# Loading the first x chunk half by plain load with TensorE transposes and half by a transposing load, with one W1 slab on ScalarE's queue

## The chip, the cores and the metric

The kernel runs on one core of one Trainium2 chip, written directly in Bass: each engine has its own list of instructions, and every order between engines is a semaphore wait. The metric is the device time in microseconds of one execution; before the change it is 147.2 us, the median of 6 runs (146.67 to 147.51).

## The reference

Two branches work on the same x and are mixed by a gate for each row. Cut to what matters:

```python
# x: 2048 x 512 bf16; wqkv: 512 x 1536; w_phi: 32 x 16 x 16; w1: 512 x 1376; w2: 1376 x 512; wo: 512 x 512
g = sigmoid((x * gate_w).sum(-1, keepdims=True))
# a: linear attention, 32 heads of 16
q, k, v = split(x @ wqkv)
pq, pk = q @ w_phi, k @ w_phi                               # for each head
phi_q = concat([softmax(pq), softmax(-pq)])                 # 32 features; phi_k alike
o = (phi_q @ (phi_k.T @ v)) / (phi_q @ phi_k.sum(0) + 1e-6)
a = o @ wo
# b: dense layer with relu
b = relu(x @ w1) @ w2
out = g * a + (1 - g) * b
```

## The kernel before, in words

x is worked on in 4 chunks of 512 rows. TensorE contracts over the partitions, so every product with x needs x transposed: tile XT holds, for each of the four 128-column blocks of x (the contraction slabs, index `dt` or `t`), all 2048 rows along the free dimension. Chunks 1 to 3 arrive in XT by a transposing load (L188). Chunk 0 is needed first and goes another way: four plain loads (L162, semaphores x00 to x03) bring its rows into XS, which is part of tile OT, so that each partition holds one row of each load. TensorE then transposes 16 blocks of 128x128 by a matmul with an identity matrix (`xtr`, L237), and VectorE (L247) and ScalarE (L249) copy the results from PSUM to XT (`xev`). A block (dt, j) is column block dt of the rows of load j. The rows are dealt out as `(p j)`: load j takes rows 4p+j, and the output rows of the first four tiles are stored back by the same rule (`orow`).

The first large piece of TensorE work is the first 8 column units of h = x @ w1 for chunk 0 (`slab`, L520). Here the slab of the contraction is the outer loop: slab(0) runs units 0 to 7 into eight PSUM banks, then slab(1), slab(2) and slab(3) add to them; each is 8 matmuls of 512 columns. Slab t needs W1 rows t*128 to t*128+127 (events w10a, w10, w11, w12, w13; slab 0's row block comes as two halves) and XT's column block t of chunk 0 (events xv..., list `XV`). After slab 3 the relus (L258, L260) free the banks, and the remaining units of W1 (`hunit`, L272), the v tiles (`vtile`, L404) and the folded q/k weights (`pre`, L306) follow without a pause in the order written out by hand.

All loads sit on two queues, each in the order written: SyncE (SP) issues x00, x02, then w10a, w10, w11, w12, w13 (L165), the rest of W1 (w1r, L178), w_phi (wps, L180), the v weights (wv, L182), two transposing loads of the q and k weights (wqk0, wqk1, L185), and the transposing loads of chunks 1 to 3 (x1 to x3, L188). ScalarE (ACT) issues x01, x03 and the gate vector (gr, L170). `warm` (L231) issues matmuls on a constant that keep TensorE busy while the first x rows are on their way. `p.early` places an engine's first instructions ahead of the start barrier.

Of the kernel before, what the change touches and what calls it, by code (L numbers as in the profile page):

```python
# [68 lines left out]
def bass_gated_mix__linear_kernel_hedgehog__dense_activation_relu__prompt_kernel(  # L69
# [11 lines left out]
    x2 = A_x.rearrange("b s d -> (b s) d")  # L81
    o2 = out.rearrange("b s d -> (b s) d")
# [3 lines left out]
    DFF = B_w1.shape[1]  # L86
    P = 128
    NT = S // P
    NDT = D // P
# [15 lines left out]
    with ExitStack() as es:  # L105
        E = es.enter_context
        XT = E(nc.sbuf_tensor("XT", [P, NDT, S], BF16))
# [43 lines left out]
        p = _Plan(["sp", "pool", "act", "dve", "pe"])  # L151
        free = {b: [] for b in range(8)}


        xq = x2[0:512, :].rearrange("(p j) d -> p j d", j=4)
        oq = o2[0:512, :].rearrange("(p j) d -> p j d", j=4)

        def orow(m):
            return oq[:, m, :] if m < 4 else o2[m * P:(m + 1) * P, :]

        def loadx0(j, eng):
            p.dma(eng, lambda e: e.dma_start(out=XS[:, j, :], in_=xq[:, j, :]), f"x0{j}", ev=f"x0{j}")  # L162

        def loadw1(t, c0=0, c1=DFF, tag=""):
            p.dma("sp", lambda e: e.dma_start(  # L165
                out=W1[:, t, c0:c1], in_=B_w1[t * P:(t + 1) * P, c0:c1]), f"w1{t}{tag}", ev=f"w1{t}{tag}")

        for j in range(NDT):
            loadx0(j, ("sp", "act")[j % 2])
        p.dma("act", lambda e: e.dma_start(out=GR[0:NDT, :], in_=gate_w.rearrange("(j p) -> j p", p=P)),  # L170
              "gr", after=["grz"], ev="gr")
        p.early("act")
        p.early("sp")
        loadw1(0, 0, 4 * P, "a")
        loadw1(0, 4 * P, 8 * P)
        for t in range(1, NDT):
            loadw1(t, 0, 8 * P)
        p.dma("sp", lambda e: e.dma_start(  # L178
            out=W1[:, :, 8 * P:DFF], in_=B_w1[:, 8 * P:DFF].rearrange("(j p) n -> p j n", p=P)), "w1r", ev="w1r")
        p.dma("sp", lambda e: e.dma_start(  # L180
            out=WPS[:, :, :], in_=A_w_phi.rearrange("(g hl) r c -> (hl r) g c", g=NDT)), "wps", ev="wps")
        p.dma("sp", lambda e: e.dma_start(  # L182
            out=WV[:, :, :], in_=A_wqkv[:, 2 * D:3 * D].rearrange("(j p) n -> p j n", p=P)), "wv", ev="wv")
        for i in range(2):
            p.dma("sp", lambda e, i=i: e.dma_start_transpose(  # L185
                out=WQKT[:, 4 * i:4 * i + 4, :], in_=A_wqkv[:, i * D:(i + 1) * D]), f"wqk{i}", ev=f"wqk{i}")
        for c in range(1, NCH):
            p.dma("sp", lambda e, c=c: e.dma_start_transpose(  # L188
                out=XT[:, :, c * 512:(c + 1) * 512], in_=x2[c * 512:(c + 1) * 512, :]), f"x{c}", ev=f"x{c}")
# [9 lines left out]
            after=["wps"], ev="wd")  # L199
        for gt in range(NDT):  # L200
# [4 lines left out]
                after=["wd", "m8"], ev=f"wbd{gt}")  # L205
# [11 lines left out]
             after=["r64"], ev="m32")  # L217

        def xready(c):
            return [f"xv{n}" for n in ("a0", "a1", "a2", "c0", "d0", "b1", "b3")] if c == 0 else [f"x{c}"]  # L220

        def gatecol(bank):
            gp = PS[:, bank, 0:NDT]
# [5 lines left out]
        def warm(n, cols=512):  # L229
            for _ in range(n):  # L230
                p.op("pe", lambda e: e.matmul(PS[:, 4, 0:cols], ones[:, 0:P], ones[:, 0:cols], start=True, stop=True),  # L231
                     after=["one"])

        def xtr(nm, blocks, bank, last=True, off=0):
            for i, (dt, j) in enumerate(blocks):
                o = off + i * P
                p.op("pe", lambda e, dt=dt, j=j, o=o: e.matmul(  # L237
                    PS[:, bank, o:o + P], XS[:, j, dt * P:(dt + 1) * P], IDN[:, :], start=True, stop=True),
                    after=["idn", f"x0{j}"] + (free[bank] if o == 0 else []),
                    ev=(f"xt{nm}" if last and i == len(blocks) - 1 else None))  # L240

        def xev(eng, nm, js, dts, bank):
            w = len(js) * P
            d = XT[:, dts[0]:dts[-1] + 1, js[0] * P:js[0] * P + w]
            s = PS[:, bank, 0:len(dts) * w].rearrange("p (t c) -> p t c", c=w)
            if eng == "dve":
                p.op("dve", lambda e: e.tensor_copy(d, s), after=[f"xt{nm}"], ev=f"xv{nm}")  # L247
# [21 lines left out]
        def hunit(c, kt, eng="act", bank=None):  # L269
            bank = nextbank() if bank is None else bank  # L270
            for t in range(NDT):
                p.op("pe", lambda e, t=t: e.matmul(  # L272
                    PS[:, bank, :], W1[:, t, kt * P:(kt + 1) * P], XT[:, t, c * 512:(c + 1) * 512],
                    start=(t == 0), stop=(t == NDT - 1)),
                    after=(xready(c) + w1all + free[bank] if t == 0 else ()),
                    ev=(f"h{c}_{kt}" if t == NDT - 1 else None))
            relu(c, kt, bank, eng)
# [224 lines left out]
        def comb(m, cs=slice(0, 512), tag="", eng="sp"):  # L502
            ob = m % 3
            bank = fbank[(m, tag)]
            n = cs.stop - cs.start
            p.op("dve", lambda e: e.scalar_tensor_tensor(  # L506
                out=OSB[:, ob, cs], in0=PS[:, bank, 0:n], scalar=OMG[:, m:m + 1],
                in1=TFA[:, m % 2, cs], op0=ALU.mult, op1=ALU.add),
                after=[f"fb{m}{tag}", f"ta{m}"] + ([f"out{m - 3}"] if m >= 3 else []), ev=f"cb{m}{tag}")
            free[bank] = [f"cb{m}{tag}"]  # L510
            p.dma(eng, lambda e: e.dma_start(out=orow(m)[:, cs], in_=OSB[:, ob, cs]),
                  f"out{ob}" if m < NT - 3 else "fin", after=[f"cb{m}{tag}"], ev=f"out{m}{tag}")


        UB = (3, 4, 5, 0, 6, 7, 2, 1)
        XV = (("xva0", "xvc0", "xvd0"), ("xva1", "xvb1"), ("xva2", "xvb1"), ("xva2", "xvb3"))

        def slab(t):
            for u in range(8):
                p.op("pe", lambda e, u=u: e.matmul(  # L520
                    PS[:, UB[u], :], W1[:, t, u * P:(u + 1) * P], XT[:, t, 0:512],
                    start=(t == 0), stop=(t == NDT - 1)),
                    after=["w10a" if t == 0 and u < 4 else f"w1{t}", *XV[t]] + (free[UB[u]] if t == 0 else []),
                    ev=(f"h0_{u}" if t == NDT - 1 else None))

        A, B = (0, 1), (2, 3)
        warm(4)
        p.early("pe")
        warm(1, 384)
        xtr("a0", ((0, 0),), 6, last=False)  # L530
        xtr("a1", ((1, 0),), 5, last=False)
        xtr("a2", ((2, 0),), 7, last=False)
        xtr("a2", ((3, 0),), 7, last=False, off=2 * P)
        xtr("a0", ((0, 1),), 6, off=P)
        xtr("a1", ((1, 1),), 5, off=P)
        xtr("a2", ((2, 1),), 7, last=False, off=P)
# [47 lines left out]
        for m in range(NT):  # L584
# [33 lines left out]
        for m in range(NT):  # L618
            if m > 1 and m + 3 < NT:
                nd(m + 3)  # L620
            if m + 1 < NT - 1:
                finB(m + 1, FB[(m + 1) % 3])
            if m == 1:
                nd(m + 3)
            if m == 0:
                nd(2)
                nd(3)
            finA(m, (6, 2, 0)[max(m - NT + 3, 0)])
            if m < NT - 1:
                comb(m)  # L630
        m = NT - 1
# [3 lines left out]
        for i, cs in enumerate(cuts):  # L635
            comb(m, cs, "ab"[i], ("sp", "act")[i])
# [35 lines left out]
```

The softmax here doesn't subtract the row's maximum and nothing guards it: scores larger than these inputs give would overflow.

## Time and profile before

| | |
|---|---|
| runs before | 147.2 us median, 146.67 to 147.51 |
| the profiled execution: its own time | 146.77 us |
| its span, first to last instruction | 145.5 us |
| TensorE (PE) busy | 141.8 us, 97% of the span |
| VectorE (DVE), ScalarE (ACT), GpSimd (POOL) busy | 92.4, 72.7, 52.0 us |
| granted TensorE clock | 1.00 |
| first x load lands, first slab matmul starts | 2.76 us, 4.69 us |
| the slab stage (32 matmuls), then the next group | 4.69 us, 11.75 us |

The page has one line for each engine's busy time, a strip of 40 slices over the span, the DMA queues, the chain of work that ended last, and the costliest groups of instructions with what ended their idle time. "L520" is line 520 of the kernel before. Other views of the same trace used here are the chain in order of time, the waits of one engine, one line's instructions with the time from issue to landing of its DMAs, and the DMA packets in a window. All times are us from the first instruction of the span.

### The profile page before, as it was taken

Reading aid. Unit: us, or ns where it says so; the run is one execution under the profiler, and the core shown is the slowest. Engines: PE = TensorE matmul, PEld = TensorE weight load, DVE = VectorE, ACT = ScalarE, POOL = GpSimd, SP = SyncE. Lnnn points to the kernel's source line nnn. Section 1 sums busy time; section 2 is a strip of 40 time slices with the busy share of each in tenths; the row PEclk is TensorE's granted clock in tenths of the full one; section 3 lists DMA queues with packets and bytes.
Section 4 is the critical chain, followed back from the end, with each engine's and each line's share of the span. In section 5 each row is a group of like instructions: output and inputs, shape, how many; then the busy total and the mean of one; then the engine's idle time right before and its main releaser. Section 6 shows DMA issues by size and latency. Waiting matters only on the chain.

```text
span 145.5 us, 2522 instructions
## 1 busy us (share of the span) xinstructions
PE 141.8 (97%) x960; PEld 72.8 (50%) x977; DVE 92.4 (64%) x158; ACT 72.7 (50%) x125; POOL 52.0 (36%) x62
## 2 busy tenths in 40 slices
PE   8999999999999999999999999999999999999994
PEld 3444744444446555544645555554444444444443
DVE  2528818777686888678698968664455555555342
ACT  3315667779778778797878861022211111111150
POOL 2040004777878668678879810200000000000000
DMA  6999990213459973325734332355242222322213
GB/s 182 312 257 226 267 182 17 54 26 68 72 118 360 147 203 66 71 46 110 77 72 98 82 72 39 75 106 132 53 108 72 72 72 70 79 72 74 72 45 106
DMA packets 45509, 16.12 MB, mean 111 GB/s; under 512 B 39384, under 2 KB 45112, under 8 KB 45496
## 3 DMA queue, kind: packets, MB, share of 16 engines
q1 hardware_dynamic: 45056, 15.65, 48.0%
q10 hardware_dynamic: 440, 0.30, 0.6%
q8 instruction: 8, 0.13, 0.4%
q14 instruction: 5, 0.04, 0.1%
HBM read 4.41 MB, written 2.10 MB: 45 GB/s over the span
## 4 chain that ended last, share of the span: by engine, by line
PE 95%; DMA 2%; DVE 1%; issue 1%; SPq 0%
PE PS L483 26%; PE PS L272 19%; PE PS L328 18%; PE PS L492 9%; PE PS L404 9%; PE PS L520 5%; PE PS L458 3%; PE PS L426 3%; PE PS L284 2%; DMA OT<-in_A_x_dram 2%; PE PS L306 1%; DVE WQK L506 1%; DVE XT L247 1%; PE PS L237 0%; SPq L657 0%
## 5 line engine op out<-in xcount | busy, mean ns | idle before, releaser
L483 PE MATMUL PS<-W,HT 128*128 128x512 bf16 (+3 forms) x182 | 40.2, 366 | 0.3
L372 POOL TENSOR_TENSOR EB<-EB,SC 128x1024 bf16<-128x1024 bf16 x15 | 28.9, 1928 | 23.8 <-DVE SC L370 23.8
L348 ACT ACTIVATE EB<-PS 128x480 bf16<-128x480 f32 (+1 forms) x44 | 30.1, 757 | 14.2 <-PE PS L328 14.2
L497 ACT ACTIVATE TFA<-PS,GT 128x512 bf16<-128x512 f32 x16 | 11.0, 687 | 42.7 <-PE PS L492 36.6
L272 PE MATMUL PS<-XT,W 128*128 128x512 bf16 x124 | 30.2, 379 | 0.2
L328 PE MATMUL PS<-WQK,XT 128*128 128x480 bf16 x128 | 28.5, 366 | 0.0
L368 DVE TENSOR_REDUCE ZB<-EB 128x64 f32<-128x1024 bf16 x15 | 18.3, 1220 | 14.2 <-ACT EB L348 14.2
L506 DVE SCALAR_TENSOR_TENSOR WQK<-PS,OMG,TFA 128x512 bf16<-128x512 f32 (+2 forms) x17 | 12.2, 719 | 23.6 <-ACT TFA L497 22.4
L483 PEld LDWEIGHTS PS<-W,HT 128*128 128x128 bf16 (+1 forms) x187 | 17.0, 98 | 17.4
L258 ACT ACTIVATE HT<-PS 128x512 bf16<-128x512 f32 x35 | 20.3, 616 | 6.8 <-PE PS L520 5.0
L328 PEld LDWEIGHTS PS<-WQK,XT 128*128 128x128 bf16 x128 | 12.5, 98 | 13.6
L383 DVE TENSOR_REDUCE ZB<-EB 128x64 f32<-128x1024 bf16 x16 | 18.7, 1168 | 0.0
L272 PEld LDWEIGHTS PS<-XT,W 128*128 128x128 bf16 x128 | 12.0, 98 | 13.2
L392 POOL TENSOR_TENSOR EB<-EB,SC 128x512 bf16<-128x512 bf16 x16 | 16.9, 1055 | 1.3
L492 PE MATMUL PS<-WO,OT 128*128 128x512 bf16 x62 | 16.0, 378 | 0.1
L404 PE MATMUL PS<-WV,XT 128*128 128x512 bf16 x59 | 15.3, 378 | 0.3
L468 DVE TENSOR_TENSOR WQK<-PS,RDEN 128x512 bf16<-128x512 f32 x16 | 11.1, 691 | 0.6
L492 PEld LDWEIGHTS PS<-WO,OT 128*128 128x128 bf16 x64 | 6.1, 97 | 7.2
L414 ACT ACTIVATE VS<-PS 128x512 bf16<-128x512 f32 x14 | 8.5, 610 | 2.0 <-PE PS L404 2.0
L370 DVE RECIPROCAL SC<-ZB 128x64 f32<-128x64 f32 x16 | 8.8, 553 | 0.5
L404 PEld LDWEIGHTS PS<-WV,XT 128*128 128x128 bf16 x64 | 5.4, 97 | 4.8
L458 PEld LDWEIGHTS PS<-KVNZ,PHQ 128*128 128x128 bf16 x128 | 6.1, 97 | 3.6
(57 smaller groups left out, 86.8 us busy)
## 6 DMA issues: line engine op xcount, KB each, us to landing
out_dram<-WQK SPq DMA_DIRECT2D x15, 128.0 KB, 1.7
W<-in_B_w_dram SPq DMA_DIRECT2D x3, 256.0 KB, 4.8
W<-in_B_w_dram SPq DMA_DIRECT2D x2, 384.0 KB, 5.4
WV<-in_A_wqkv_dram SPq DMA_DIRECT2D x1, 512.0 KB, 6.2
W<-in_B_w_dram SPq DMA_DIRECT2D x1, 512.0 KB, 4.5
WO<-in_A_wo_dram SPq DMA_DIRECT2D x2, 256.0 KB, 3.5
W<-in_B_w_dram SPq DMA_DIRECT2D x1, 352.0 KB, 5.7
OT<-in_A_x_dram SPq DMA_DIRECT2D x2, 128.0 KB, 2.8
```

The source lines that it names most:

```text
L258: p.op("act", lambda e: e.activation(dst, src, ACT.Relu), after=[f"h{c}_{kt}"], ev=ev)
L272: p.op("pe", lambda e, t=t: e.matmul(PS[:, bank, :], W1[:, t, kt * P:(kt + 1) * P], XT[:, t, c * 512:(c + 1) * 512], start=(t == 0), stop= ...
L328: p.op("pe", lambda e, dt=dt, which=which: e.matmul(PS[:, which, 0:DE], XT[:, dt, m * P:(m + 1) * P], WQK[:, which, dt * DE:(dt + 1) * DE] ...
L348: p.op("act", lambda e: e.activation(dst, s_, ACT.Exp, scale=scale), after=[f"qk{m}"] + busy, ev=ev)
L368: p.op("dve", lambda e: e.tensor_reduce(zk, ek, AX.X, ALU.add), after=[emk, f"cst{b}"], ev=f"zk{m}")
L372: p.op("pool" if m < NT - 1 else "dve", lambda e: e.tensor_tensor(EB[:, b, 3, :].rearrange("p (g f) -> p g f", f=DH), EB[:, b, 2, :].rearr ...
L383: p.op("dve", lambda e: e.tensor_reduce(ZB[:, b, 0:64].rearrange("p (h s) -> p h s", s=2), bass.AP(tensor=EB, offset=base, ap=[[EBS, P], [ ...
L392: p.op("pool", lambda e: e.tensor_tensor(EB[:, b, 0, :].rearrange("p (h s f) -> p h s f", h=H, s=2)[:, :, 1, :], EB[:, b, 1, :].rearrange( ...
L404: p.op("pe", lambda e, dt=dt: e.matmul(PS[:, bank, :], XT[:, dt, m * P:(m + 1) * P], WV[:, dt, :], start=(dt == 0), stop=(dt == NDT - 1)), ...
L483: p.op("pe", lambda e, kt=kt, M=M: e.matmul(PS[:, bank, 0:n], HT[0:M, kt, m * P:(m + 1) * P], W2[0:M, kt, cs], start=(kt == 0), stop=(kt = ...
L492: p.op("pe", lambda e, t=t: e.matmul(PS[:, bank, :], OT[:, t, m * P:(m + 1) * P], WO[:, t, :], start=(t == 0), stop=(t == NDT - 1)), after ...
L506: p.op("dve", lambda e: e.scalar_tensor_tensor(out=OSB[:, ob, cs], in0=PS[:, bank, 0:n], scalar=OMG[:, m:m + 1], in1=TFA[:, m % 2, cs], op ...
```

## The change

Only the first x chunk and the order of the first loads change.

- x chunk 0 is dealt out as `(j p)`: row block j is rows 128j to 128j+127, and the output rows are stored in plain order (`orow` goes).
- Two plain loads on SP instead of four on two queues: each brings two row blocks, and only the first 256 of the 512 columns.
- Column blocks 2 and 3 of the chunk (256 columns, 512 rows) come to XT by one transposing load, event x0t, on SP between w11 and w13.
- w12 leaves SP's queue; ScalarE issues it after its two copies of the transposed blocks.
- TensorE transposes 8 blocks instead of 16; the copies are VectorE a0 and d0, ScalarE c0 and a1, instead of four on VectorE and three on ScalarE. One matmul of `warm` (384 columns) stands between the last transpose and slab(0).
- slab(1) waits for a1, slabs 2 and 3 for x0t.

```diff
-        xq = x2[0:512, :].rearrange("(p j) d -> p j d", j=4)
-        oq = o2[0:512, :].rearrange("(p j) d -> p j d", j=4)
-        def orow(m):
-            return oq[:, m, :] if m < 4 else o2[m * P:(m + 1) * P, :]
-        def loadx0(j, eng):
-            p.dma(eng, lambda e: e.dma_start(out=XS[:, j, :], in_=xq[:, j, :]), f"x0{j}", ev=f"x0{j}")
-        def loadw1(t, c0=0, c1=DFF, tag=""):
+        xq = x2[0:512, :].rearrange("(j p) d -> p j d", j=4)
+        def loadx0(h):
             p.dma("sp", lambda e: e.dma_start(
+                out=XS[:, 2 * h:2 * h + 2, 0:2 * P], in_=xq[:, 2 * h:2 * h + 2, 0:2 * P]), f"x0{h}", ev=f"x0{h}")
+        def loadw1(t, c0=0, c1=DFF, tag="", eng="sp"):
+            p.dma(eng, lambda e: e.dma_start(
                 out=W1[:, t, c0:c1], in_=B_w1[t * P:(t + 1) * P, c0:c1]), f"w1{t}{tag}", ev=f"w1{t}{tag}")
-        for j in range(NDT):
-            loadx0(j, ("sp", "act")[j % 2])
+        for h in range(2):
+            loadx0(h)
...
         loadw1(0, 0, 4 * P, "a")
         loadw1(0, 4 * P, 8 * P)
-        for t in range(1, NDT):
-            loadw1(t, 0, 8 * P)
+        loadw1(1, 0, 8 * P)
+        p.dma("sp", lambda e: e.dma_start_transpose(
+            out=XT[:, 2:4, 0:512], in_=x2[0:512, 2 * P:4 * P]), "x0t", ev="x0t")
+        loadw1(3, 0, 8 * P)
...
-        XV = (("xva0", "xvc0", "xvd0"), ("xva1", "xvb1"), ("xva2", "xvb1"), ("xva2", "xvb3"))
+        XV = (("xva0", "xvc0", "xvd0"), ("xva1",), ("x0t",), ("x0t",))
...
-        A, B = (0, 1), (2, 3)
         warm(4)
         p.early("pe")
         warm(1, 384)
-        xtr("a0", ((0, 0),), 6, last=False)
...
-        xtr("a2", ((3, 1),), 7, off=3 * P)
+        xtr("a0", ((0, 0), (0, 1)), 6)
+        xtr("a1", ((1, 0), (1, 1)), 7, last=False)
         xtr("c0", ((0, 2),), 2)
-        xtr("d0", ((0, 3),), 0)
-        xev("dve", "a0", A, (0,), 6)
-        xev("dve", "a1", A, (1,), 5)
+        xtr("d0", ((0, 3),), 1)
+        xtr("a1", ((1, 2), (1, 3)), 7, off=2 * P)
+        xev("dve", "a0", (0, 1), (0,), 6)
         xev("act", "c0", (2,), (0,), 2)
-        xev("dve", "d0", (3,), (0,), 0)
-        xev("act", "a2", A, (2, 3), 7)
-        xtr("b1", [(dt, j) for dt in (1, 2) for j in B], 1)
-        xtr("b3", [(3, j) for j in B], 6)
-        xev("act", "b1", B, (1, 2), 1)
-        xev("dve", "b3", B, (3,), 6)
+        xev("dve", "d0", (3,), (0,), 1)
+        xev("act", "a1", (0, 1, 2, 3), (1,), 7)
+        loadw1(2, 0, 8 * P, eng="act")
+        warm(1, 384)
         slab(0)
```

More of the change, by code (lines that the diff above doesn't have):

```diff
@@ L219, in xready @@
         def xready(c):
-            return [f"xv{n}" for n in ("a0", "a1", "a2", "c0", "d0", "b1", "b3")] if c == 0 else [f"x{c}"]
+            return ["xva0", "xvc0", "xvd0", "xva1", "x0t"] if c == 0 else [f"x{c}"]
         def gatecol(bank):
@@ L238, in xtr @@
                     PS[:, bank, o:o + P], XS[:, j, dt * P:(dt + 1) * P], IDN[:, :], start=True, stop=True),
-                    after=["idn", f"x0{j}"] + (free[bank] if o == 0 else []),
+                    after=["idn", f"x0{j // 2}"] + (free[bank] if o == 0 else []),
                     ev=(f"xt{nm}" if last and i == len(blocks) - 1 else None))
@@ L510, in comb @@
             free[bank] = [f"cb{m}{tag}"]
-            p.dma(eng, lambda e: e.dma_start(out=orow(m)[:, cs], in_=OSB[:, ob, cs]),
+            p.dma(eng, lambda e: e.dma_start(out=o2[m * P:(m + 1) * P, cs], in_=OSB[:, ob, cs]),
                   f"out{ob}" if m < NT - 3 else "fin", after=[f"cb{m}{tag}"], ev=f"out{m}{tag}")
         UB = (3, 4, 5, 0, 6, 7, 2, 1)
-        XV = (("xva0", "xvc0", "xvd0"), ("xva1", "xvb1"), ("xva2", "xvb1"), ("xva2", "xvb3"))
+        XV = (("xva0", "xvc0", "xvd0"), ("xva1",), ("x0t",), ("x0t",))
         def slab(t):
@@ L529, in bass_gated_mix__linear_kernel_hedgehog__dense_activation_relu__prompt_kernel @@
         warm(1, 384)
-        xtr("a0", ((0, 0),), 6, last=False)
[L531 to L536, printed above, removed]
-        xtr("a2", ((3, 1),), 7, off=3 * P)
+        xtr("a0", ((0, 0), (0, 1)), 6)
+        xtr("a1", ((1, 0), (1, 1)), 7, last=False)
         xtr("c0", ((0, 2),), 2)
-        xtr("d0", ((0, 3),), 0)
-        xev("dve", "a0", A, (0,), 6)
-        xev("dve", "a1", A, (1,), 5)
+        xtr("d0", ((0, 3),), 1)
+        xtr("a1", ((1, 2), (1, 3)), 7, off=2 * P)
+        xev("dve", "a0", (0, 1), (0,), 6)
         xev("act", "c0", (2,), (0,), 2)
-        xev("dve", "d0", (3,), (0,), 0)
-        xev("act", "a2", A, (2, 3), 7)
-        xtr("b1", [(dt, j) for dt in (1, 2) for j in B], 1)
-        xtr("b3", [(3, j) for j in B], 6)
-        xev("act", "b1", B, (1, 2), 1)
-        xev("dve", "b3", B, (3,), 6)
+        xev("dve", "d0", (3,), (0,), 1)
+        xev("act", "a1", (0, 1, 2, 3), (1,), 7)
+        loadw1(2, 0, 8 * P, eng="act")
+        warm(1, 384)
         slab(0)
```

## The prediction

> **What bounds the kernel now.** I read the page's engine shares first, then the chain of work that ended last.
>
> ```profile
> PE 141.8 (97%) x960; PEld 72.8 (50%) x977; DVE 92.4 (64%) x158; ACT 72.7 (50%) x125; POOL 52.0 (36%) x62
> PE 95%; DMA 2%; DVE 1%; issue 1%; SPq 0%
> ```
>
> TensorE is busy for 97% of the span and is 95% of the chain. Behind the first slab matmul the chain is almost only TensorE, so a change outside its matmuls can gain or lose only where TensorE still waits: at the start. The chain in order of time, cut to its first 12 us:
>
> ```profile
> 0.08 2.68 DMA OT<-in_A_x_dram
> 2.76 0.14 issue
> 2.90 0.71 PE PS L237 x5
> 3.61 0.02 issue
> 3.63 0.96 DVE XT L247 x3
> 4.59 0.09 issue
> 4.69 6.21 PE PS L520 x28
> 10.89 0.05 issue
> 10.94 0.81 PE PS L520 x3
> 11.75 1.73 PE PS L272 x8
> ```
>
> The columns are start and length. The first x load takes until 2.76, transposes follow, then three VectorE copies in a row (a0, a1, d0), and slab(0) starts at 4.69. From there nothing waits: 32 slab matmuls at 0.2155 us are 6.90 us, so the next group issues at 11.59. (It is shown from 11.75, where the modelled ends of pipelined matmuls part.) Slab t starts at 4.69 + 1.724 t: 6.41, 8.14, 9.86. These are the marks: the change gains what it brings these four starts forward, and of that only what is left at the last.
>
> The W1 loads are close behind. The waits of TensorE's weight loads have
>
> ```profile
> PEld PS L520 <- DMA W<-in_B_w_dram: 0.8, 3, 0.3
> ```
>
> which cost nothing here, since weight loads run ahead of the matmuls. But the landings in the trace are tight: w10a 4.47, w10 5.49 (needed at 5.55), w11 6.25 (6.41), w12 7.18 (8.14), w13 7.86 (9.86). A slab that starts earlier soon runs into its weights unless these come forward too.
>
> For the transposing loads I read two lines and their time from issue to landing. The first pair is L185, 512 KB each from HBM, behind all the plain loads; the second is L397, 256 KB each, on a quiet queue.
>
> ```profile
> L185 SPq DMA_TRANSPOSE PHQ<-in_A_wqkv_dram x2: 2217/3814/5410, 5.1 to 10.5; - x2
> DMA to landing us min/median/max: 4.7/6.3/7.9
> ```
>
> ```profile
> L397 SPq DMA_TRANSPOSE PHQ<-EB x16: 1232/1232/1735, 27.2 to 91.9; - x16
> DMA to landing us min/median/max: 2.7/2.7/5.0
> ```
>
> The reader is to see that the same instruction holds SP for 1.23 us when nothing is ahead of it, and held it 5.41 us at 5.05, where the wv load drained only at 10.6. x0t, of 256 KB, lies between these.
>
> [...] the x loads, two on SP and two on ACT, landed one after the other at 2.76, 3.11, 3.44 and 3.95. So w12 on ACT gets no bandwidth of its own. [...] the transposes start 107 ns apart up to 3.71 and 55 ns apart from 4.08. The slabs now start in full clock; an earlier one may not.
>
> **The change part by part.**
>
> *x loads.* Half the bytes lie ahead of W1. The last three of the four 128 KB loads landed 0.40 us apart on average ((3.95 - 2.76)/3), so 256 KB less is 0.80 us. The runs in HBM shrink from 1 KB to 512 B: in the trace's packets 1 KB takes 46 ns and 256 B takes 18 ns, so 512 B is about 27 (estimate, on the line through both); 32 packets an engine at 27 instead of 16 at 46 gives back 0.13. W1's landings come forward by about 0.66: w10a 3.81, w10 4.83, w11 5.59. x00 has no ACT load interleaved with it: 16 packets at 27 instead of 16 at 46 ns ahead of its landing, 2.76 - 0.30 = 2.45; x01 0.43 later, 2.9. The ACT issues of x go; gr is issued earlier. Nobody waits for that.
>
> *Transposes and copies.* Warm-up holds TensorE until 2.4. Two a0 and two a1 transposes at 107 ns run from 2.55 to 2.98, c0 and d0 from 3.0, the last two a1 to 3.42, and the 384-column warm matmul (0.32 us at half clock) to 3.74. A copy starts some 0.24 to 0.31 after its last transpose (3.39 to 3.63 in the trace): a0 on VectorE 2.97 to 3.40 (0.42), then d0 3.44 to 3.72 (0.28); c0 on ScalarE 3.34 to 3.62, behind its table load, which ends at 3.10. a1 leaves VectorE's row, 0.33 us of its pace, and goes to ScalarE as one 512-column copy of 0.6, done at 4.3, needed by slab 1 at 5.6. The eight transposes and the copies a2, b1, b3 that disappear lay partly beside other work; their gain is inside these times. So slab(0) can start near 3.80 by its data, 3.85 by w10a: 0.84 earlier. If the full clock comes at about 4.05 as now, 0.2 us runs at half speed, a loss of 0.10.
>
> *Slabs 0 and 1.* w10 is needed at 4.81 and due at 4.83, w11 needed at 5.67 and due at 5.59. No loss to 0.2.
>
> *x0t and w12, for slab 2 at 7.40.* SP issues x0t at about 2.42, in w12's old place. After w11 at 5.59 its 256 KB need 1.05 us (the L397 transfers moved 0.26 MB in that time) and about 0.35 to land: 6.99 alone. w12 is issued by ScalarE behind a1's dispatch, between 3.8 and 4.3; a first packet follows an issue by 1.0 to 1.3 (0.08 to 1.1, and 0.21 to 1.5), so at about 5.3. It shares with x0t, and its 256 KB take 0.7 to 0.9: both are there by 7.84 at the latest of this reckoning. Slab 2 therefore waits 0 to 0.45. Lower bound below nothing: no, a new wait cannot bring work forward. Upper bound: L185's 7.9 us from issue, 10.3. I take 0.25. Behind ScalarE's issue (0.43 us) stands nothing until the relus at 10.3.
>
> *SP's order behind it.* The transpose holds SP for 1.23 us against w12's 0.43: w13, w1r, wps, wv, wqk0 are issued 0.8 later[...]. In bytes the stream up to w13 is the same but for the slower transposing and the short packets, 0.3 to 0.5 us. w13 lands near 8.3 against 9.3 needed; w1r 9.5 against 11.1; wv 11.1 against 13.0; wqk0 13.4 against 14.7; wqk1 15.7 against the fifth `pre` at 16.4 (now 15.2 and 16.9). wps, behind which GpSimd builds Wbd until 11.2, has 3 us. x1 17.6 against 20.4. All covered; the thinnest cover is wqk1's 0.7.
>
> *Stores.* The four first output tiles go to contiguous rows; they end long before TensorE's last work: nothing.
>
> **Sum:** 0.84 - 0.10 (clock) - 0.25 (x0t, w12) = about 0.5 us gained, between 0.3 and 0.75. The profiled execution, 146.77 with a span of 145.5, would be 146.3. It lies 0.43 below the median of 147.2; the median goes to 146.7.
>
> **Rivals.**
>
> *R1, x0t takes the place of the wait removed (slower).* Its issue is held until the plain loads ahead drained on the slowest DMA engine, as wqk0's was. It decides from the point where x0t or w12 lands after 8.14, slab 2's present start; each us beyond is lost in full. With L185's 7.9 us, x0t lands at 10.3: 2.2 us later than now, 149.4. A middle case, half of the queue to wait for, lands near 8.8: 147.9. For it speaks the 5.41 us row. Against it: only 0.77 MB of loads are issued on SP ahead of x0t, 2.1 MB ahead of wqk0 (x00, x02, W1, wps and wv).
>
> *R2, the gain is eaten at the start (within 0.3%).* The slow w10 step (1.02 us for 128 KB) or a late clock takes 0.3 to 0.5: in an execution where the full clock comes at 5.5, slab(0) started 0.84 earlier gains only 0.42. Together with the x0t wait 0.1 to 0.4 remain: 147.0. The spread of the runs, 0.84 us, may come from that clock; nothing in one trace shows it.
>
> *R3, weights bound all along.* If W1's landings don't move, slab(0) starts at 4.5: 147.1, within 0.3%. Unlikely, since landings follow the bytes ahead.
>
> **Numbers.** 0.3%, 0.44 us, is about what a measurement of this kernel can tell from no change. My forecast has 0.50 and lies above that bound; R2 and R3 have 0.28; R1 has 0.22, mostly its middle case. The range runs from 146.0 (no wait at x0t, and noise in the median of 0.2) to 147.8 (a little short of R1's middle case); some 2 in 10 lie outside.
>
> **What would show it.** Right: the first slab matmul near 3.85, slab 2 near 7.6, the group after the slabs at about 11.1 instead of 11.59, and everything behind it shifted by the same. Wrong: a TensorE wait inside L520's line on DMA XT or W of over 0.5; an x0t issue of 3 us or more; slab matmuls 0.43 us apart past 4.2; or a new wait on wqk1 near 16.4.

## The result, and the profile after

The changed kernel takes 147.64 us (median of 37 runs, 146.96 to 151.2); the kernel before, run beside it, takes 146.96 (74 runs, 146.52 to 149.56). The ratio is 1.0041, with a 95% interval of 1.0028 to 1.0055: slower, by a little more than the 0.3% that the prediction took for the least that can be told. Ratios, here and below, leave out the slow runs, those over 1.5% above the fastest of their kernel (7 of these 37), while medians count all. The forecast was 146.7.

The first profiled execution is one of the longest of the changed kernel, 150.86 us with a span of 149.6; so I show a second one beside it, of 147.10 us with a span of 145.8 (after_fourth in the experiments). From the page of the long one, its engine shares, its granted clock over 40 slices and its chain:

```profile
PE 143.4 (96%) x953; PEld 72.8 (49%) x970; DVE 91.8 (61%) x156; ACT 72.4 (48%) x124; POOL 52.0 (35%) x62
PEclk9995999999999999999999999999999999999999
PE 93%; DMA 5%; issue 1%; DVE 1%; DVEq 0%; ACT 0%
```

The same lines of the second one, without the clock:

```profile
PE 142.5 (98%) x970; PEld 72.3 (50%) x970; DVE 91.7 (63%) x156; ACT 72.3 (50%) x124; POOL 52.2 (36%) x62
PE 95%; DMA 3%; DVE 1%; issue 0%; DVEq 0%; ACT 0%
```

TensorE is as busy as before, but the DMA share of the chain has grown from 2% to 3% and 5%. Where that is, the timeline of TensorE shows; its columns are start, length, engine, line, tiles, count, and in brackets the idle time ahead with what ended it. First the long execution:

```profile
4.30 3.70 PE L519 MATMUL PS<-XT,W 128*128 128x512 bf16 x16 [0.29 <-DMA W<-in_B_w_dram]
10.52 5.31 PE L519 MATMUL PS<-XT,W 128*128 128x512 bf16 x16 [2.52 <-DMA W<-in_B_w_dram]
```

Then the second:

```profile
3.30 0.53 PE L230 MATMUL PS<-ONE 128*128 128x384 bf16 x1
3.72 3.73 PE L519 MATMUL PS<-XT,W 128*128 128x512 bf16 x16
8.46 3.63 PE L519 MATMUL PS<-XT,W 128*128 128x512 bf16 x16 [1.00 <-DMA W<-in_B_w_dram]
```

The reader is to see that the one run of 32 slab matmuls of before has become two of 16, with a hole between slab 1 and slab 2. The first half starts where the prediction wanted it (3.72 against 3.85). The second starts at 8.46, later than the 8.14 of before. In the long execution the hole is 2.5 us, and the matmuls behind it run at half clock once more (slab 2 and slab 3 take 5.31 instead of 3.63; start to start they are twice as far apart from 11.31 to 14.72). The chain of the second execution names the load that ends the hole (start, length, what):

```profile
3.52 0.02 issue
3.54 0.01 ACT XT L248
3.55 4.86 DMA W<-in_B_w_dram
8.41 0.05 issue
8.46 3.63 PE PS L519 x16
12.09 1.08 PE PS L271 x5
```

It is w12: ScalarE issues it at 3.55, right as it dispatches the a1 copy (L248), and it lands 4.86 us later, at 8.41. x0t was there at 6.15. The two issues, from the views of their lines (mean issue time in ns, its place, then the landing):

```profile
L174 SPq DMA_TRANSPOSE XT<-in_A_x_dram x1: 1334/1334/1334, 2.5 to 2.5; - x1
DMA to landing us min/median/max: 3.6/3.6/3.6
```

```profile
L162 ACTq DMA_DIRECT2D W<-in_B_w_dram x1: 365/365/365, 3.5 to 3.5; - x1
```

The transposing load holds SP for 1.33 us, as forecast (1.23). So R1's picture of an x0t that is held at its issue is not what happened.

**From slab 2 to the end.** In 13 profiles of 9 kernels the time of the execution is the start of slab 2 plus 138.64 us, within 0.02: 146.77 with 8.14 (before), 146.50 with 7.86 (before, a second profile), 147.10 with 8.46, 146.71 with 8.05, 149.16 with 10.52 (a kernel below). So the first 8 us decide, and two profiles can be compared by three marks: slab 0, slab 2, and where TensorE reaches full clock. Executions that stop again later don't obey it: the long one (150.86, 1.70 above it, its second half-clock stretch) and the kernels below that wait at `pre`. Read backwards, the medians put slab 2 at 8.3 before (146.96) and at 9.0 after (147.64).

### The profile page after: what moved, and what is told of

It reads as the page before. It is cut to its first block, busy times and chain, and to the rows that moved or that the text cites. A ratio compares the mean times of both kernels' runs of the same rounds, so it can differ in the third digit from the quotient of the medians.

```text
span 149.6 us, 2504 instructions
## 1 busy us (share of the span) xinstructions
PE 143.4 (96%) x953; PEld 72.8 (49%) x970; DVE 91.8 (61%) x156; ACT 72.4 (48%) x124; POOL 52.0 (35%) x62
## 4 chain that ended last, share of the span: by engine, by line
PE 93%; DMA 5%; issue 1%; DVE 1%; DVEq 0%; ACT 0%
PE PS L482 25%; PE PS L271 18%; PE PS L327 17%; PE PS L491 9%; PE PS L403 9%; DMA W<-in_B_w_dram 5%; PE PS L519 4%; PE PS L457 3%; PE PS L425 3%; PE PS L283 2%; PE PS L230 1%; PE PS L305 1%; PE PS L236 1%; DVE WQK L505 1%; DVE ONE L206 0%
## 5 line engine op out<-in xcount | busy, mean ns | idle before, releaser
L271 PE MATMUL PS<-XT,W 128*128 128x512 bf16 x123 | 30.1, 379 | 0.3
L519 PE MATMUL PS<-XT,W 128*128 128x512 bf16 x32 | 9.0, 446 | 2.8 <-DMA W<-in_B_w_dram 2.8
```

The lines of the kernel that those rows point to most:

```text
L271: p.op("pe", lambda e, t=t: e.matmul(PS[:, bank, :], W1[:, t, kt * P:(kt + 1) * P], XT[:, t, c * 512:(c + 1) * 512], start=(t == 0), stop= ...
L519: p.op("pe", lambda e, u=u: e.matmul(PS[:, UB[u], :], W1[:, t, u * P:(u + 1) * P], XT[:, t, 0:512], start=(t == 0), stop=(t == NDT - 1)), ...
```

## The experiments

The letters in the quoted expectations stand for the theories that they name. Five questions were asked in turn: which of the two moved loads it is, whether ScalarE's queue matters, whether the transposing does, what comes next when slab 2 is early, and what makes the spread. All medians and ratios are gathered in the table at the end of this part.

### Which load, and where it stands

The changed kernel again (label after_again):

> The changed kernel once more, beside the kernel before on the same chip, for a second profile. Theory M (mixing: plain packets of ScalarE's queue that meet the packets of a transposing load on SyncE's queue nearly stop the DMA engines): a stretch of 1 to 3 us with under 60 GB/s begins when w12's first packets meet x0t's, at about 5.2 us; x0t lands after 7.5, w12 lands last, after 8.2; 147.2 to 148.5 us. Theory Q (a transposing load amid a full SyncE queue is slow by itself): the same landing of x0t, but the slow stretch begins with x0t's own packets at 4.3 us, and w12 is only a bystander. Theory D (nothing is slow, the bytes ahead just add up): x0t at 7.0, w12 at 7.8, 146.7 us.

147.54, ratio 1.0049: the result repeats. Its profile (147.05) has slab 2 at 8.40, w12 at 8.14 and no wait for it there; what delays slab 2 in it is the clock (below), though with w12 at 8.14 it could hardly have started earlier than before. A stretch under 60 GB/s, as M has it, isn't in this profile: from 5.5 to 6.5 us it has 221 GB/s.

w12 back on SP's queue, directly behind x0t:

```
             out=XT[:, 2:4, 0:512], in_=x2[0:512, 2 * P:4 * P]), "x0t", ev="x0t")
+        loadw1(2, 0, 8 * P)
...
-        loadw1(2, 0, 8 * P, eng="act")
```

> Only w12 moves: back to SyncE's queue, directly behind x0t. M: no plain packet of another queue meets x0t; x0t lands near 6.9, w12 near 7.9 and w13 near 8.6, slab 2 starts before 8.2, and the kernel is 0.2 to 0.5 us faster than before (146.5 to 146.8). Q: x0t lands at 8.5 to 9.2 as in the changed kernel and w12 behind it later still, 148 us or more. D: the same as the changed kernel.

147.01, ratio 1.0002. In its profile w12 still lands at 8.51, 1.9 us after x0t (6.63), so the profile is no better (slab 2 at 8.55); none of the three theories has this. Two of the sixteen DMA engines make it so late, the others had their part of w12 there by 7.51. But of 14 runs none is above 147.5, where half of the changed kernel's are. Away from ScalarE the long runs go; in the one profile, w12 behind the transposing load stays late.

The same with w12 ahead of x0t:

```
         loadw1(1, 0, 8 * P)
+        loadw1(2, 0, 8 * P)
         p.dma("sp", lambda e: e.dma_start_transpose(
...
-        loadw1(2, 0, 8 * P, eng="act")
```

> w12 on SyncE's queue directly ahead of x0t. M: w12 lands near 6.3, x0t near 7.7, no slow stretch; slab 2 waits 0 to 0.2 us; 146.5 to 146.8. Q: x0t still takes 6 us or more from issue, lands at 9 or later; 148. D: as M, since the bytes are the same.

146.83, ratio 0.9993. w12 lands at 6.54, x0t at 7.59, slab 2 starts at 7.72, close to the 7.6 that was forecast. The gain isn't kept: the chain (start, length, what) reads

```profile
12.07 4.98 DMA PHQ<-in_A_wqkv_dram
17.05 0.05 issue
17.10 1.01 PE PS L306 x16
18.11 0.69 PE PS L284 x16
```

wqk1 lands at 17.05, and the fifth `pre`, which the early slabs now bring up at about 16.3, waits for it: the time is 0.77 us above slab 2's start plus 138.64.

w12 first of all on ScalarE's queue, behind gr:

```
+        loadw1(2, 0, 8 * P, eng="act")
         p.early("act")
...
-        loadw1(2, 0, 8 * P, eng="act")
```

> w12 stays on ScalarE's queue but is issued at the start, behind the gate vector, so that its packets pass before x0t's begin at about 4.3. M: w12 lands near 4.5, x0t near 6.9 without a slow stretch; the price is that w12's 256 KB go ahead of or beside w10a, w10 and w11, which land 0.5 to 0.9 later, so slab 0 starts at 4.6 to 5.0; 146.8 to 147.3. Q: x0t lands at 8.5 or later whatever w12 does; 148. A third theory, A (ScalarE's queue is served badly against SyncE's): w12 lands after 7 although it is issued at 1 us.

148.54, ratio 1.0043, 19 runs from 146.63 to 149.56: a miss. w12 is issued at 1.03 and lands at 4.14, ahead of w10a (4.53) and w10; x01 lands only at 3.63; so slab 0 starts at 4.58 instead of 3.8; with full clock only from 7.11 in its profile, slab 2 is at 9.28. That accounts for the profiled 147.91. What makes its runs above 148 I did not find.

### ScalarE's queue alone

To take x0t out of it, I moved w12 to ScalarE in the kernel before, behind the b1 copy:

```
-        for t in range(1, NDT):
-            loadw1(t, 0, 8 * P)
+        loadw1(1, 0, 8 * P)
+        loadw1(3, 0, 8 * P)
...
         xev("act", "b1", B, (1, 2), 1)
+        loadw1(2, 0, 8 * P, eng="act")
```

> The kernel before with one edit: w12 on ScalarE's queue, behind its last copy, no transposing load near it. Theory M' (a plain load on ScalarE's queue is slow, and in some runs very slow, where it meets a transposing load of SyncE's queue): w12 lands between 7.2 and 8.2, no run above 148 beyond the one in twenty that the kernel before has too, 146.8 to 147.1 us. Theory A' (ScalarE's queue delays w12 by itself): w12 lands after 8.5 in the profile, median 147.4 or more and a tail of runs above 148.

149.33, ratio 1.0158 (1.0115 to 1.0201): far outside the noise, with no x0t in the kernel at all. The chain:

```profile
4.56 5.92 DMA W<-in_B_w_dram
10.47 0.05 issue
10.52 2.76 PE PS L520 x12
```

w12 is issued at 4.56, when SP has already issued w13, w1r, wps and wv (the last from 3.92 to 4.43) and has just begun with wqk0 (4.47). It lands at 10.47, 5.92 us later. The DMA view shows how. Queue q1 is SP's, q10 ScalarE's; the columns are packets, MB, share of 16 engines. From 4.6 to 7.7 us:

```profile
DMA packets 1409, 0.86 MB, mean 279 GB/s; under 512 B 569, under 2 KB 1261, under 8 KB 1409
q1 hardware_dynamic: 1409, 0.86, 101.9%
```

From 7.7 to 9.5:

```profile
q1 hardware_dynamic: 563, 0.40, 79.9%
q10 hardware_dynamic: 135, 0.25, 36.5%
```

For 3.1 us all 1409 packets are SP's and none is w12's. w12's first packets come at 7.9, when w13, w1r and wps are through and wv is under way, and from there the two queues move side by side. What holds them back until then, the trace doesn't show. If it is what SP issued earlier, w12 needs only to be issued earlier than SP's next loads. So I held SP, in this same kernel, until b1 is copied:

```
         loadw1(1, 0, 8 * P)
+        p.wait("sp", ["xvb1"])
         loadw1(3, 0, 8 * P)
```

> The kernel before with w12 on ScalarE's queue, as before_w12_act, and SyncE holding back w13 and all its later loads until the copy b1 is done (about 5.2), so that w12, issued at about 4.6, stands ahead of them. Theory F (a load is served in the order of issue over both queues: it waits for all that SyncE has issued before it): w12 lands near 6.8 instead of 10.5, slab 2 is not held, and 146.9 to 147.3 us, the rest being the later w13 and weights. Theory A' (ScalarE's queue itself is slow or served last): w12 again lands after 9, 149 us.

147.08, ratio 1.0001: 2.2 us come back by a wait that only delays other loads. The DMA view from 4.9 to 7 us:

```profile
q10 hardware_dynamic: 144, 0.26, 41.9%
q1 hardware_dynamic: 51, 0.10, 16.5%
W<-in_B_w_dram ACTq DMA_DIRECT2D x1, 256.0 KB, 2.6
```

Same queue, same place on ScalarE, 2.6 us to landing instead of 5.9; the first packet follows the issue by 1.0 us instead of 3.4. So ScalarE's queue doesn't make w12 late by itself; what SP has issued ahead of it does.

The reverse: in the changed kernel w12 as late as can be, issued only when x0t has landed, and slab 2 made the last of the four.

```
-        loadw1(2, 0, 8 * P, eng="act")
+        p.dma("act", lambda e: e.dma_start(
+            out=W1[:, 2, 0:8 * P], in_=B_w1[2 * P:3 * P, 0:8 * P]), "w12", after=["x0t"], ev="w12")
...
-        for t in range(1, NDT):
+        for t in (1, 3, 2):
```

> w12 on ScalarE's queue, but issued only when x0t has landed, so that the two never meet; the slabs run in the order 0, 1, 3, 2 so that W1's slab 2 is needed last. M': x0t lands near 6.7, w12 is issued then and lands near 9.0, just ahead of the last slab (9.0 to 9.7); no tail above 148; 146.7 to 147.1. A': tail above 148 as in the changed kernel.

155.06, ratio 1.0268: a miss by far. The issue, at 6.36, stands behind SP's wv and just behind wqk0's issue, which begins at 6.13. Its first packets come at 9.9, and then they run beside wqk0's until 15.9. Its row in the DMA view (KB, us to landing) and the wait of slab 2:

```profile
W<-in_B_w_dram ACTq DMA_DIRECT2D x1, 256.0 KB, 10.1
```

```profile
PE PS L519 <- DMA W<-in_B_w_dram: 6.1, 1, 6.1
```

And the changed kernel with w12's issue moved forward on ScalarE, to the landing of x00, between SP's issues of w11 and x0t (a small ScalarE operation ahead of it is meant to bring the table load forward, 1.28 us in the profile before):

```
+        p.op("act", lambda e: e.activation(OMG[:, 0:1], ONE[:, :], ACT.Copy), after=["one"])
+        p.dma("act", lambda e: e.dma_start(
+            out=W1[:, 2, 0:8 * P], in_=B_w1[2 * P:3 * P, 0:8 * P]), "w12", after=["x00"], ev="w12")
...
-        loadw1(2, 0, 8 * P, eng="act")
```

> The changed kernel with w12 on ScalarE's queue, issued as soon as x00 has landed (about 2.5), so between SyncE's issues of w11 and x0t; ScalarE's table load is brought ahead by a small copy into a tile that is overwritten later. F: w12 lands between 6 and 7, as on SyncE's queue ahead of x0t, no tail above 148, 146.7 to 147.0. A': w12 lands after 8, a tail above 148, 147.4 or more.

146.91, ratio 0.9992. Issued at 2.35, w12 lands at 5.91 and x0t at 7.07; slab 2 starts at 7.24 in its profile (146.28, the shortest of all profiles), which would be 145.88 by 138.64, if `pre` did not wait for wqk1:

```profile
10.96 5.24 DMA PHQ<-in_A_wqkv_dram
16.20 0.05 issue
16.25 1.01 PE PS L305 x16
```

Its packets (4.22 to 5.57) stand between those of w11 and those of x0t (5.08 to 6.48), in the order of issue, though w12 is on another queue. So with w12 issued ahead of x0t, on either engine, both are there by 7.1 to 7.6, within the forecast's 7.84.

### The transposing of x0t

x0t as a plain load of the same bytes (256 rows as they lie, not transposed), first in the changed kernel:

```
-        p.dma("sp", lambda e: e.dma_start_transpose(
-            out=XT[:, 2:4, 0:512], in_=x2[0:512, 2 * P:4 * P]), "x0t", ev="x0t")
+        p.dma("sp", lambda e: e.dma_start(
+            out=XT[:, 2:4, 0:512], in_=x2[0:256, :].rearrange("(p a) d -> p a d", a=2)), "x0t", ev="x0t")
```

> The changed kernel with x0t as a plain load of the same 256 KB (256 rows of x in their own order instead of 512 half rows transposed, so column blocks 2 and 3 of the first chunk hold other numbers); w12 still on ScalarE's queue. M': x0t lands near 6.3 and w12 near 7, no tail above 148; slab 2 is not held by DMA; the kernel gains what the clock leaves, 0.3 to 0.6 us: 146.3 to 146.6. A': a tail above 148 as in the changed kernel, median 147.2 or more.

147.91, ratio 1.0039, 12 of 22 runs above 147.8: without any transposing load ahead of it the changed kernel is as slow, and its long runs stay. So a transposing load near w12 isn't needed for them, against M'; A' fell with before_w12_act_hold. SP is free 0.65 us earlier and issues w13 at 3.26, ahead of ScalarE's w12 at 3.63; w13 starts to land at 6.10, w12 at 7.08, complete at 8.27. Their packets run side by side (5.08 to 7.7 and 5.26 to 7.75), so this edit changed two things, the transposing and w12's place behind w13.

Then with w12 on SP ahead of the plain x0t:

> All W1 slabs on SyncE, w12 ahead of x0t, and x0t a plain load of the same bytes (256 rows of x in their own order, so column blocks 2 and 3 of the first chunk hold other numbers). Theory W (what is left of the gain after w12's return is lost because the transposing load lengthens the stream of loads by 1 to 1.5 us up to wqk1): w13 lands near 7.5, wqk1 near 15.6 instead of 17.0, TensorE no longer waits for it; 146.2 to 146.6, 0.3 to 0.5 below w12_sp_ahead. If the clock alone takes the gain: no difference to w12_sp_ahead (146.8).

146.73, ratio 0.998 (0.9966 to 0.9994), 0.1 to 0.2 us below w12_sp_ahead where 0.3 to 0.5 was expected, and the two intervals overlap. In its profile wqk1 lands at 16.79 here too, where 15.6 was expected. One DMA engine is late (w13 lands from 6.71 to 9.25), so it isn't shown that the transposing is what lengthens the stream. This kernel does not do the transposition and is no candidate.

### What is late next

Both are made from the kernel with w12 ahead of x0t on SP (the diffs are against it), and both are meant to give wqk1 more time: first `rest(0)`, then v tile 3, ahead of the second half of `pre`.

```
+        rest(0)
         for i in range(4, 8):
             pre(i)
-        rest(0)
```

> All W1 slabs on SyncE's queue with w12 ahead of x0t, and TensorE's rest(0) (0.69 us) moved ahead of the second half of pre. Theory W (of that order's early start, what the clock leaves is lost again at wqk1, which landed at 17.05 where TensorE was ready at about 16.3): the moved work covers 0.69 of that wait; 0.3 to 0.5 us faster than without the move, 146.3 to 146.5. If wqk1 is not what took the gain: no difference to 146.8.

147.05, ratio 0.9986: nothing that can be told apart. The move uncovers a copy that lay hidden:

```profile
17.64 0.22 PE PS L306 x4
17.87 0.02 issue
17.89 0.67 DVE WQK L311
18.56 0.05 issue
```

```
+        vtile(3)
         for i in range(4, 8):
             pre(i)
...
-            if m + 3 < NT:
+            if 0 < m and m + 3 < NT:
```

> All on SyncE with w12 ahead of x0t, and TensorE computes v tile 3 (0.86 us) ahead of the second half of pre instead of behind the first q/k tile; rest(0) stays between pre and the q/k tile, where it covers the copies. W: the wait for wqk1 is covered; 146.4 to 146.6, and below the kernel before by 0.2% or more. If not: 146.8 as w12_sp_ahead.

148.11, ratio 1.0084: worse. v tile 3 uses the PSUM bank of v tile 2 and waits 0.70 for its copy (L412), and later TensorE waits 1.84 for ScalarE's EB (L348). The order of work behind the slabs is tight on all sides; none of this bears on the result itself.

### The spread

18 of the 37 runs of the changed kernel are above 147.8, and two edits tried to find why. SP held behind x0t until a1 is copied, so that w13 comes well after w12:

```
             out=XT[:, 2:4, 0:512], in_=x2[0:512, 2 * P:4 * P]), "x0t", ev="x0t")
+        p.wait("sp", ["xva1"])
         loadw1(3, 0, 8 * P)
```

> The changed kernel with SyncE holding w13 and all behind it until the copy a1 is done (about 4.3), so that nothing but x0t can be ahead of w12, which ScalarE issues at about 3.7 inside x0t's issue (2.55 to 3.89). Race of issue: the tail above 147.8 goes, median 146.9 to 147.1. Meeting of packets: the tail stays, median 147.4 or more.

147.32, ratio 1.0039, 3 of 17 runs above 147.8: w12 lands at 8.62, no better, with 97 GB/s from 5.5 to 6.5 us. Then also w12 itself only after a1 (issued at 4.17, behind the whole issue of x0t), and w13 behind it:

```
+        p.wait("sp", ["dm"])
         loadw1(3, 0, 8 * P)
...
-        loadw1(2, 0, 8 * P, eng="act")
+        p.dma("act", lambda e: e.dma_start(
+            out=W1[:, 2, 0:8 * P], in_=B_w1[2 * P:3 * P, 0:8 * P]), "w12", after=["xva1"], ev="w12")
+        p.op("act", lambda e: e.activation(OMG[:, 0:1], ONE[:, :], ACT.Copy), after=["one"], ev="dm")
```

> The changed kernel with w12 issued by ScalarE only after its copy a1 (about 4.4), when SyncE's issue of x0t has ended, and SyncE holding w13 until w12 has been issued: w12 neither meets x0t nor has w13 ahead of it. Both theories: w12 lands near 7.3, no tail, 146.8 to 147.2. If the tail stays here too, neither of the two is its cause.

147.14, ratio 1.0017 (0.9994 to 1.0039): w12 lands at 7.53, but 6 of 22 runs are still above 147.8. So neither the overlap of the two issues nor w13 is the whole cause of the long runs. They are fewer than the changed kernel's 18 of 37 in both, so each edit may take some of them away; that isn't settled.

Four single profiles, to see more than one execution of each:

> The kernel before once more, for the clock. Theory C: full clock comes [...] between 3.8 and 7.2 us; the slabs lose half of the time from 4.69 to that point, and the time is 146.5 plus that, at most 147.75.

> The changed kernel once more, for its tail. If the time is above 147.8: w12 lands after 9, either with packets of over 200 ns on both queues (meeting) or with short packets behind w13 or w1r (race). If below: w12 lands before 8.9.

> The changed kernel once more. In the nine profiles without a wait for wqk1 or a second half-clock window, the time is 138.64 us plus the start of slab 2; this one should follow that within 0.05. If it is above 147.8, slab 2 starts after 9.15 and w12 lands just ahead of it. Late order: w12's packets come behind w13's and w1r's at 300 GB/s or more. Meeting: a stretch under 100 GB/s with w12 packets of over 200 ns from 5.3 us on.

> The changed kernel once more, as after_fourth: time 138.64 us plus the start of slab 2. If above 147.8, either w12's packets stand behind w13's and w1r's (late order) or a stretch under 100 GB/s with long w12 packets follows the first ones at about 5.3 us (meeting).

They gave 146.50, 146.71, 147.10 and 147.16; none fell on a long run. The kernel before has slab 0 at 4.41 in its second profile, 0.28 earlier than in the first, and the full clock from about 3.8. (The 3.8 to 7.2 us expected of it were an estimate of mine; the 20 profiles show 3.75, or a little before, to 7.11.) Together with the first two, these are five profiles of the changed kernel, below the first one of the kernel before:

| us | slab 0 | w11 | x0t | w12, first to last engine | slab 2 | its wait | full clock from |
|---|---|---|---|---|---|---|---|
| 146.77 (before) | 4.69 | 6.25 | - | 5.46 to 7.18 | 8.14 | 0 | 4.05 |
| 146.71 | 3.69 | 5.17 | 7.14 | 6.60 to 8.01 | 8.05 | 0.43 | 4.7 |
| 147.05 | 3.82 | 5.49 | 7.29 | 7.08 to 8.14 | 8.40 | 0 | 6.16 |
| 147.10 | 3.72 | 5.17 | 6.15 | 6.70 to 8.41 | 8.46 | 1.17 | 3.98 |
| 147.16 | 3.75 | 5.33 | 7.24 | 7.00 to 8.47 | 8.51 | 1.28 | 3.75 or before |
| 150.86 | 4.30 | 5.44 | 9.16 | 8.05 to 10.47 | 10.52 | 2.68 | 4.48 |

The wait is the gap between the last start of slab 1 and the first of slab 2, less the 0.216 of a matmul. The full clock is read from the starts of successive matmuls.

Medians and ratios of the kernels:

| kernel | median (runs) | ratio to before, 95% |
|---|---|---|
| changed | 147.64 (37) | 1.0041, 1.0028 to 1.0055 |
| after_again | 147.54 (16) | 1.0049, 1.0024 to 1.0073 |
| w12_sp_behind | 147.01 (14) | 1.0002, 0.9985 to 1.0019 |
| w12_sp_ahead | 146.83 (14) | 0.9993, 0.9976 to 1.0010 |
| w12_act_first | 148.54 (19) | 1.0043, 1.0014 to 1.0072 |
| before_w12_act | 149.33 (6) | 1.0158, 1.0115 to 1.0201 |
| before_w12_act_hold | 147.08 (14) | 1.0001, 0.9981 to 1.0022 |
| w12_act_late | 155.06 (6) | 1.0268, 1.0218 to 1.0317 |
| after_act_x00 | 146.91 (22) | 0.9992, 0.9974 to 1.0009 |
| plain_x0t | 147.91 (22) | 1.0039, 1.0016 to 1.0062 |
| sp_ahead_plain | 146.73 (22) | 0.9980, 0.9966 to 0.9994 |
| sp_ahead_rest | 147.05 (14) | 0.9986, 0.9966 to 1.0005 |
| sp_ahead_vtile | 148.11 (6) | 1.0084, 1.0055 to 1.0113 |
| after_hold_w13 | 147.32 (17) | 1.0039, 1.0018 to 1.0060 |
| after_apart | 147.14 (22) | 1.0017, 0.9994 to 1.0039 |

The kernel before had medians of 146.94, 146.97, 146.98 and 146.80 in the four groups in which these were run. No version that does the whole computation is faster than before by what can be told.

## Why the prediction was wrong

**x loads, transposes and copies: right.** Slab 0 starts at 3.69 to 3.82 in four of five profiles, against 3.85 forecast and 4.69 and 4.41 in the two profiles before; w11 lands at 5.17 to 5.49 against 5.59. Of the 0.84, 0.6 to 1.0 were there.

**x0t's issue and landing: right in four of five.** 1.33 us on SP, landed at 6.15 to 7.29 (6.99 forecast).

**"It shares with x0t, and its 256 KB take 0.7 to 0.9: both are there by 7.84 at the latest of this reckoning": the step that failed.** The start of w12 was right: its first packet comes at 5.34 to 5.57 us in four profiles, about 5.3 forecast. Its length was not: from there to the landing 2.6 to 3.1 us pass. The reckoning has only x0t beside w12. In the traces x0t is nearly through when w12 starts, and w12 runs beside what SP issued right behind it, w13 and then w1r. For these the sum has nothing. The DMA view of the second execution, from 5.75 to 7.75 us:

```profile
DMA packets 329, 0.51 MB, mean 253 GB/s; under 512 B 15, under 2 KB 117, under 8 KB 329
q1 hardware_dynamic: 223, 0.31, 46.5%
q10 hardware_dynamic: 106, 0.20, 40.0%
```

And a part of that time is slow. From 5.5 to 6.5:

```profile
DMA packets 90, 0.14 MB, mean 144 GB/s; under 512 B 21, under 2 KB 21, under 8 KB 90
q10 hardware_dynamic: 51, 0.09, 61.4%
q1 hardware_dynamic: 39, 0.05, 20.3%
```

In seven profiles in which w12 follows the transposing x0t, the long one apart, this microsecond has 97 to 221 GB/s. Two queues that meet aren't enough for it: with the plain x0t both queues move, in the same stretch,

```profile
DMA packets 178, 0.33 MB, mean 332 GB/s; under 512 B 6, under 2 KB 26, under 8 KB 178
q10 hardware_dynamic: 78, 0.16, 49.1%
q1 hardware_dynamic: 100, 0.17, 48.9%
```

Nor are two queues needed: w12_sp_behind, with one alone, has 211 GB/s. But not every change from a transposing load to a plain one is slow: in after_act_x00 w13 follows x0t at 320 GB/s (6.25 to 7.25).

How much of the delay is the slow microsecond, and how much the sharing with w13, is not separated. With the plain x0t, without the slow microsecond, w12 beside w13 still lands at 8.27; with the transposing x0t and w13 held until w12 has been issued (after_apart) it lands at 7.53. Shown, by one profile for most of the kernels, is that w12's place matters, by about 1 us: issued ahead of x0t, the pair is there by 6.96 to 7.62 (six profiles); behind it, by 8.01 to 8.62 in seven and by 7.53 in after_apart, the long execution and w12_act_late apart.

From w11's landing to the last of the pair 2.65 to 3.25 us pass in four profiles (5.0 in the long one), where my sum had 2.25 (7.84 - 5.59). So R1's point, "x0t or w12 lands after 8.14", was reached or nearly, but by w12 and not by the mechanism that R1 names. I took 0.25 us for this wait, within 0 to 0.45; it was 0, 0.43, 1.17 and 1.28, and 2.68 in the long execution.

That w12 shares with x0t from its first packet on was an estimate of mine. Two loads that have both started do run side by side in the trace of after_fourth (w12 from 5.35 to 7.94, w13 from 5.45 to 8.34). When a load's turn begins does not follow from that: in before_w12_act w12 moved nothing for 3.1 us behind SP's earlier loads, and in after_apart, issued at 4.17 instead of 3.55, it starts at 5.26 all the same, when x0t runs out. The trace of before could not tell sharing from plain order of issue. Its x loads were issued at 0.08, 0.21, 0.54 and 0.62 and landed in that order, at 2.76, 3.11, 3.44 and 3.95; both give that.

**The clock, 0.10: mis-sized.** I took the full clock to come at about 4.05 as in the one trace, and had the late case as R2. Over the 20 profiles it comes anywhere from 3.75, or a little before, to 7.11. That is a range of 3.4 us; what sets the point within it is not shown. Matmuls ahead of it start 0.43 us apart instead of 0.2155, so half of what lies between slab 0 and the full clock is lost: (6.16 - 3.82)/2 = 1.17 in the execution of 147.05, where slabs 0 and 1 took 4.58 instead of 3.45, 1.13 more. An estimate from these numbers: if it falls evenly over 3.75 to 7.11 in both kernels, the mean loss is 0.44 for a slab 0 at 4.69 and 0.79 at 3.85, so the earlier start loses 0.35, not 0.10. The five profiles of the changed kernel lost 0, 0.1, 0.1, 0.5 and 1.2. The spread of the kernel before is about as wide: (7.11 - 4.69)/2 is 1.21, and 73 of its 74 runs lie between 146.52 and 147.80, within 1.28.

**SP's order behind it: right for the changed kernel, too tight for the gain.** wqk1 lands at 15.9 to 16.7 in four profiles (15.7 forecast, 15.2 before). With slab 2 this late nobody waits for it. In w12_sp_ahead and after_act_x00, where slab 2 is early, `pre` waits: the cover of 0.7, which I called the thinnest, is gone.

**The sum.** By slab 2 the gain is gone. It starts at 8.05 to 8.51 in the four profiles of usual length, where the prediction wanted 7.6 and the two profiles before have 8.14 and 7.86. w12's landing holds it in three of them, the clock in the fourth. The two losses don't add up: w12's load doesn't wait for the slabs, so a late clock hides its wait. These four profiles are runs of 146.71 to 147.16, all below the median of 147.64, so they don't account for the whole difference of 0.68 between the medians; the rest belongs to the long runs, whose cause is open. R3 fell: the weights came forward.

**What stays open** is the upper half of the runs. Half of them are above 147.8, where slab 2 would be past 9.1; one profile of five fell there. Six of the seven runs above 149 have that profile's granted clock of 0.989, the other 1.000; a second half-clock stretch (1.70 of a span of 149.6) is just this 1.1%, so it probably stands in those six and makes the longest of them. But it follows on the late w12, it doesn't explain it. The profile shows, from 5.5 to 7.25 us,

```profile
DMA packets 99, 0.04 MB, mean 21 GB/s; under 512 B 93, under 2 KB 93, under 8 KB 99
q1 hardware_dynamic: 93, 0.02, 114.1%
q10 hardware_dynamic: 6, 0.01, 8.1%
```

that is, 99 packets in 1.75 us whose own times fill all sixteen engines, with single packets of x0t and w12 taking 500 to 1850 ns. The long runs go away when w12 is on SP's queue (none of 14 above 147.8, behind x0t or ahead of it), or issued by ScalarE just ahead of x0t (none of 22, after_act_x00). They do not when w13 is held, nor when the two are issued apart, and a plain x0t has them as well (22 runs up to 148.84). Whether all the long runs have such a stretch isn't shown, and what the engines wait for in it I could not tell.

## What to carry to other kernels

Before moving a load's issue to another engine, list what the other engines will have issued by then, what they issue right behind it, and how many bytes each is: here the first set when the moved load started (its first packet 3.4 us after its issue in before_w12_act, 1.0 with SP held), and the second shared the way with it (w13 in after_fourth). Of a plain and a transposing load that the same stage needs, it paid here to issue the plain one first (the pair there by 6.96 to 7.62, and by 7.53 to 8.62 the other way round). And an early start is worth what the next two deadlines leave of it: here the clock took some 0.35 of 0.84 by the estimate above, and where w12 was in time, the wait for wqk1 took 0.4 (after_act_x00) to 0.8 (w12_sp_ahead).

## What the runs showed of the hardware

- In before_w12_act w12, issued by ScalarE at 4.56, moved its first packet 3.4 us later, behind loads that SyncE had issued earlier; with SyncE held (before_w12_act_hold) it came 1.0 us after the issue. Once w12 had started, it ran side by side with w13, which SyncE issued later (w12 from 5.35 to 7.94, w13 from 5.45 to 8.34 in after_fourth).
- Where w12 followed the transposing load of 256 KB, a microsecond had 97 to 221 GB/s in seven profiles (97 in after_hold_w13, 144 in after_fourth, 221 in after_again), and 1.75 us had 21 GB/s in an eighth, the long execution; where it followed a plain load of the same bytes, the microsecond had 332 GB/s in one (plain_x0t).
- Issued beside a transposing load of 512 KB and behind wv, a plain load of 256 KB took 10.1 us in w12_act_late; from 10 to 13 us the DMA engines moved 113 GB/s together.
- The point from which matmuls start 0.2155 us apart instead of 0.43 lay between 3.75 us, or a little before, and 7.11 us in the 20 profiles. Half of what of that range lies behind the slab 0 of before (4.69) is 1.21 us, against a spread of 1.28 in 73 of the 74 runs of that kernel.
- In the long execution a hole of 2.5 us in TensorE's work was followed, 0.8 us after it, by 3.4 us of half clock (11.31 to 14.72), which cost 1.70 us. Holes of 1.2 and 1.3 us (after_fourth, after_fifth) were not, nor was one of 1.9 in the profile of before_w12_act. After one of 6.1 us (w12_act_late) the first matmuls already started 0.43 us apart.
